# Normalising the second half of x during the projections, and spreading a stack's transfers over every second pair of maximum tiles

## The chip, the cores and the metric

The kernel runs on one core of a Trainium2 chip. A core has TensorE (PE, matmuls), VectorE (DVE), ScalarE (ACT), GpSimd (POOL) and SyncE (SP, which here only issues transfers), each with its own instruction stream that runs in order, an on-chip memory of 128 partitions, PSUM banks into which PE accumulates, and 16 DMA engines for transfers to and from DRAM. The metric is the device time of one execution in microseconds (us), less is better. Before the change it is 1792.7 us, the median of 3 runs (1792.57 to 1793.63).

## The reference

A block of multi-head attention and a token mixer, mixed by a gate. x is 2048 tokens by 640 channels, with 32 heads of 20 channels; the mixer's hidden width is 1728.

```python
def _A_ref(x, wqkv, wo):
    qkv = (x @ wqkv).reshape(B, S, 3, H, Dh).transpose(2, 0, 3, 1, 4)
    q, k, v = qkv[0], qkv[1], qkv[2]
    scores = jnp.einsum("bhqd,bhkd->bhqk", q, k) * (Dh ** -0.5)
    p = _softmax(scores, axis=-1)
    o = jnp.einsum("bhqk,bhkd->bhqd", p, v)
    return o.transpose(0, 2, 1, 3).reshape(B, S, D) @ wo

def _B_ref(x, w1, b1, w2, b2):
    h = _layernorm(x, axis=-1)
    u = _gelu(jnp.einsum("bsd,sf->bdf", h, w1) + b1)
    y = jnp.einsum("bdf,fs->bds", u, w2) + b2
    return y.transpose(0, 2, 1)

g = _sigmoid((x * gate_w).sum(-1, keepdims=True))
return g * _A_ref(...) + (1 - g) * _B_ref(...)
```

The change concerns h, the normalised x, in channels 320 to 639, and the order in which some operands are brought in.

## The kernel before

Every matmul that must be exact is done in three passes on a value split into a high and a low part (`hi_lo`: ACT rounds the high part, POOL or DVE subtracts for the low part). The program goes through four stages.

Projections (up to about 220 us of the profile): q, k and v from x. `qk_unit(m, q)` is one unit of 15 matmuls into one PSUM bank; four banks take turns, so a unit's bank is needed again four units later. ACT evicts the high part `evh`, DVE the low part `evl`, and SP stores both to DRAM. The last 24 units (n = 0 to 23) carry the preparation of the mixer's first half: for each tile t of 128 tokens, SP loads channels 0 to 319 of x (`h_load`, unit t + 1), POOL normalises them (`h_norm`, unit t + 2: add the negative mean, times the reciprocal deviation), ACT and POOL split them (`h_split`, unit t + 3) into `hh` and `hl`, which stay on the chip.

Mixer (about 220 to 740 us): twice, for d = 0 (channels 0 to 319) and d = 1 (320 to 639), 14 u tiles (hidden rows, one of them the 64-row tail of w1) and 16 y tiles (128 tokens each). The weights w1 and w2 come in pieces `wr` of 256 KB on SP's queue, about nine pieces ahead, and are split by ACT and POOL into `wh` and `wl` five pieces ahead. While the y tiles of d = 0 run, the second half of x is prepared: SP loads a tile (`h_load(1, t)`), DVE normalises it (`h_norm(1, t)`, 2500 ns of the planner's clock behind a y tile), ACT and POOL split it.

Into the mixer the program deals the first part of the next stage: maximum tiles. A softmax needs each query's maximum, so scores are computed once only for their maximum: PE makes a 128x512 score tile `s` (L208), ACT rectifies some of them (`s_over`, L223), and DVE takes the maxima (L214) or, in one operation, a sum and a maximum (L233). A head pair p has 128 such tiles. How many have been dealt by a step n of the mixer is set by `dve_room(n)`, a budget of DVE time that grows evenly over the mixer; during the y tiles of d = 0 it sets aside 600 ns a tile for the normalisation.

Each pair needs a stack: `load_stack` brings k and q, high and low parts, from DRAM into 120 rows, 21 transfers of 80 or 160 KB (`ks_False`, `qs_False`). In the mixer these transfers are not issued at once but put on the list `drip`, one of them taken with each pair of maximum tiles. At maximum tile 552 the stack of the attention loop's first pair (`ks_True`, `qs_True`) goes on the same list: 20 transfers, 8 of maxima from `m_d` and one of v (336 KB in runs of 168 bytes).

Attention loop (about 740 to 1745 us): scores, exponentials on ACT, probabilities times v on PE, with the remaining maximum tiles between. Then the last projection and the output.

Order: PE, ACT and DVE follow the order in which the program writes their instructions, POOL and SP too from the last 24 units on. An instruction that waits holds up all that stands behind it on its engine. A small planner (`act`, `later_on`, `settle`) orders ACT's and POOL's mixer work by due times on a clock of its own.

Of the kernel before, what the change touches and what calls it, by code (L numbers as in the profile page):

```python
# [7 lines left out]
F32 = mybir.dt.float32  # L8
F32R = mybir.dt.float32r
AF = mybir.ActivationFunctionType  # L10
OP = mybir.AluOpType
AX = mybir.AxisListType

P = 128
S, D, H, DH, F = 2048, 640, 32, 20, 1728
NP = H // 2
NT = S // P
NC = D // P
FF = 13
FT = 14  # L20
# [10 lines left out]
def gated_mix(ctx, tc, xT, x, wqk, wv0, wv1, wo, w1, w1t, b1, w2, b2, out):  # L31
# [31 lines left out]
    r_d = dram.tile([H, DH, S], F32, name="r_d")  # L63
    v_d = dram.tile([2, NT, P, 16 * VW], F32, name="v_d")
    y_d = dram.tile([S, D], F32, name="y_d")

    cp = ctx.enter_context(tc.tile_pool(name="cp", bufs=1))
    base = ctx.enter_context(tc.tile_pool(name="base", bufs=1))
# [45 lines left out]
    omg = cp.tile([P, NT], F32, name="omg")  # L114
    b2o = cp.tile([P, NT], F32, name="b2o")

    drip = []

    def load_stack(p, ks, qs, full, eng=nc.sync):
        put = eng.dma_start if eng else lambda *a: drip.append(lambda: nc.sync.dma_start(*a))  # L120
# [34 lines left out]

    s_src, st_src, v_tiles = {}, {}, {}

    def load_v(p):
        v_tiles[p] = base.tile([P, NT, NPAIR], F32, tag="v", bufs=2, name=f"v{p}")
        c0 = NPAIR * (p % 8)  # L160
        nc.sync.dma_start(v_tiles[p], v_d[p // 8, :, :, c0: c0 + NPAIR].rearrange("t p c -> p t c"))

    s_close = []

# [308 lines left out]

    def h_load(d, t):
        xm = hp.tile([P, HALF], F32, tag="xm", bufs=4, name=f"xm{d}_{t}")
        nc.sync.dma_start(xm, x[t * P:(t + 1) * P, d * HALF:(d + 1) * HALF])
        xms[d, t] = xm

    def h_norm(d, t):
        xm = xms[d, t]  # L480
        (nc.vector if d else nc.gpsimd).tensor_scalar(xm, xm, negm[:, t:t + 1], rstd[:, t:t + 1], op0=OP.add, op1=OP.mult)  # L481

    def h_split(d, t):
        xm = xms.pop((d, t))
# [60 lines left out]
    for n, (m, q) in enumerate(units):  # L545
        if n % 4 < 2 and n // 4 * 4 + 4 < len(units):
            m2 = units[n // 4 * 4 + 4][0]
            if n % 4 == 0:
                raws[m2] = w_dma(m2)
            else:  # L550
                w[m2] = load_w(m2, raws[m2])
        if n == 8:
            s_src[0] = base_stack(0, False, None)
        if 3 <= n < NT + 3:
            hs[n - 3] = h_split(0, n - 3)
        if 2 <= n < NT + 2:
            h_norm(0, n - 2)
        if 1 <= n < NT + 1:
            h_load(0, n - 1)
        if n == 17:  # L560
            w_raw(0)
            w_raw(1)
        last_stores = qk_unit(m, w[m], q)
        if n == 23:
            w_split(3)
        for _ in range(min(2, len(drip))):
            drip.pop(0)()
        if n in (18, 19):
            w_split(n - 18)
        if n in (20, 21):  # L570
            w_raw(n - 18)
        if n == 22:
            w_split(2)
            w_raw(4)
            w_raw(5)
# [17 lines left out]
    def later_on(delay, fn):  # L593
        events.append((clock[0] + delay, next(count), fn))
# [109 lines left out]
    def mlp(hs):  # L704
        k = 0
        for d in range(2):
            g, done = {}, set()
            for f in f_order:
                if d == 0 and f == f_order[-1]:
                    for i in range(3):  # L710
                        h_load(1, i)
                ps = mlp_tile(f"u{d}_{f}")
                for c in range(4):
                    wh, wl = w_need(k)
                    k += 1
                    for i in range(4):
                        force(lambda: hs.get(4 * c + i))
                        hh, hl = hs[4 * c + i]
                        ops = [(wh, hh), (wh, hl)] if f == FF else [(wh, hh), (wh, hl), (wl, hh)]
                        for n, (a, b) in enumerate(ops):  # L720
                            pair64(ps, a[:, i], b, c == i == n == 0, c == i == 3 and n == len(ops) - 1)
                            yield
                gh = gp.tile([P, HALF], F32R, tag=f"gh{f}", name=f"gh{d}_{f}")
                gl = None if f == FF else gp.tile([P, HALF], F32R, tag=f"gl{f}", name=f"gl{d}_{f}")
                u_evac(f, d, ps, gh, gl, done)
                g[f] = (gh, gl)
            for t in range(NT):
                ps = mlp_tile(f"y{d}_{t}")
                for c in range(4):
                    wh, wl = w_need(k)  # L730
                    k += 1
                    for i in range(4 if c < 3 else 2):
                        f = 4 * c + i
                        force(lambda: f in done)
                        gh, gl = g[f]
                        if f < FF:
                            for n, (a, b) in enumerate(((wh, gh), (wh, gl), (wl, gh))):
                                pair64(ps, a[:, i], b, f == n == 0, False)
                                yield
                        else:  # L740
                            nc.tensor.matmul(ps[0], wl[:TL, i], gh[:TL], start=False, stop=False)
                            pair64(ps, wh[:, i], gh, False, True)
                            yield
                y_evac(t, d, ps)
                if d and t == NT - 2:
                    act(lambda: nc.scalar.activation(eps_t, eps_t, AF.Exp), 1500, 1000, 8000)
                if d == 0:
                    if t == 0:
                        for i in range(NT):
                            hs[i] = None  # L750
                        h_norm(1, 0)
                    if t + 1 < NT:
                        later_on(2500, lambda t=t: h_norm(1, t + 1))

                    def split(t=t):
                        hs[t] = h_split(1, t)
                        if t + 3 < NT:
                            h_load(1, t + 3)

                    act(split, 370, 2000, 3000)  # L760
# [7 lines left out]

    hooks[0] = start_ahead
    FIRST = 14  # L770
    U_STEPS = (FT - 1) * 48 + 32
    DIFF, RAW, NORM = 435, 640, 600

    def dve_work(k):
        return DIFF * min(k, NDIFF * 128) + RAW * max(0, k - NDIFF * 128)

    def dve_room(n):
        norms = min(max((n - U_STEPS) / (NT * 40), 0), 1) * NT * NORM
        return (dve_work(S_AHEAD) + NT * NORM) * (n + 1 - FIRST) / (STEPS - 20 - FIRST) - norms

    first_p = {}

# [13 lines left out]
    for n, _ in enumerate(steps):  # L796
        if n == STEPS - 28:
            s_wide[0] = False
        if n in (STEPS - 22, STEPS - 16, STEPS - 10):
            first_scores((n + 22 - STEPS) // 6)  # L800
        settle(146)
        while done + 2 <= S_AHEAD and dve_work(done) < dve_room(n):
            if done == 48:
                s_src[1] = base_stack(1, False, None)
            if done == 4 * 128 + 40:
                st_src[0] = base_stack(0, True, None)
                for half in range(2):
                    load_m(0, st_src[0][1], half, lambda *a: drip.append(lambda: nc.sync.dma_start(*a)))
                drip.append(lambda: load_v(0))
            if drip:  # L810
                drip.pop(0)()
            for _ in range(2):
                s_next()
            done += 2
            settle(233)
# [345 lines left out]
```

## Time and profile before

| | |
|---|---|
| median of 3 runs | 1792.7 us |
| profiled execution: its time | 1796.82 us |
| profiled execution: its span | 1794.7 us |
| DVE normalisations (L481) in the mixer | 16, 14.1 us together |
| POOL normalisations (L481) in the projections | 16, 10.4 us together |
| DMA engines' mean busy share, 145 to 220 us | 0.85 |
| DMA engines' mean busy share, 580 to 590 us | 0.17 |

How to read the views shown below. A row of the groups gives line, engine, operation, what is written from what (buffer numbers left out), shapes and count, then busy time in us, mean ns of one, and the idle time just before with what ended it. A row of the stretches gives the bounds, the length, each engine's busy time with its instructions in brackets (PE, PE's weight loads PEld, DVE, ACT, POOL, as far as they occur), then PE's granted clock, the DMA engines' share and GB/s; cut down to one line of the program or one engine it shows fewer columns. A row of the timeline gives the start and the duration in us, and in square brackets how long the engine was idle before and what it waited for. A row of the transfers ends with the size in KB and the median us from issue to landing.

### The profile page before, as it was taken

The page shows a single profiled execution, that of the slowest core. Times are in us where ns is not written, and L with a number is a line of the kernel's source. Part 1 is how long each engine was busy: PE and PEld are TensorE (multiplying, and loading weights), DVE is VectorE, ACT ScalarE, POOL GpSimd, SP SyncE. Part 2 cuts the span into 40 slices and gives each one's busy share as a digit, 9 for nine tenths or more (in the row PEclk, how much of TensorE's full clock was granted, in tenths as well). Part 3 has the DMA queues.
Part 4 walks back from the last instruction along what each step waited for, and adds up shares of the span by engine and source line. Part 5 has one row for each costly group of instructions (what it writes and reads, how often), then busy time and mean ns, then how long its engine had stood idle before and what let it go on. Part 6 is the DMA issues. An engine that isn't in the chain of part 4 may idle for free.

```text
span 1794.7 us, 39876 instructions
## 1 busy us (share of the span) xinstructions
PE 1779.3 (99%) x14976; PEld 1113.8 (62%) x14976; DVE 1236.7 (69%) x2394; ACT 1481.1 (83%) x2534; POOL 640.7 (36%) x898
## 2 busy tenths in 40 slices
PE   9999999999999999999999999999999999999998
PEld 7998899999999999633333333333333333333388
DVE  5303289999889999777767677676777777767244
ACT  4244388887878886699999999999999999999930
POOL 1123377778877767211111111121332121212210
PEclk9999999999999999999999999999999999999999
DMA  8757876647675564325213223052363232301653
GB/s 292 241 173 245 258 188 170 161 152 193 175 180 161 144 183 142 90 57 131 59 30 82 61 68 83 18 105 70 46 138 69 52 86 59 73 13 25 216 154 125
DMA packets 157937, 222.95 MB, mean 124 GB/s; under 512 B 68590, under 2 KB 95614, under 8 KB 154318
## 3 DMA queue, kind: packets, MB, share of 16 engines
q1 hardware_dynamic: 139568, 190.74, 39.0%
q0 software_dynamic: 15440, 24.45, 5.8%
q10 hardware_dynamic: 2736, 5.21, 1.0%
q8 instruction: 118, 1.93, 0.5%
q14 instruction: 75, 0.61, 0.1%
HBM read 165.43 MB, written 54.54 MB: 123 GB/s over the span
## 4 chain that ended last, share of the span: by engine, by line
PE 93%; DVE 3%; DMA 3%; ACT 0%; issue 0%; SPq 0%; POOL 0%; ACTq 0%; DVEq 0%; POOLq 0%
PE pv L899 29%; PE st L986 20%; PE s L208 12%; PE u L48 10%; PE y L48 8%; PE qk L54 6%; PE v L54 4%; PE a L1066 3%; DVE mx L214 1%; DMA xr<-in_xT_dram 1%; DVE ov L233 1%; DVE oy L1072 1%; DVE xm L481 1%; DMA wr<-in_w_dram 0%; DMA rbl<-r_d 0%
## 5 line engine op out<-in xcount | busy, mean ns | idle before, releaser
L214 DVE TENSOR_REDUCE mx<-s 128x1 f32<-128x512 f32 x1280 | 834.4, 686 | 282.0 <-PE s L208 216.8
L1001 ACT ACTIVATE p<-st 128x512 f32<-128x512 f32 x1022 | 583.1, 657 | 1.1 <-PE st L986 1.1
L993 ACT ACTIVATE p<-st 128x1024 f32<-128x1024 f32 x511 | 552.4, 1081 | 2.8 <-PE st L986 2.2
L899 PE MATMUL pv<-p,v 128*32 128x512 f32 x4088 | 547.2, 605 | 0.0
L986 PEld LDWEIGHTS st<-qs_True,ks_True 62*128 62x128 f32 x2044 | 245.8, 184 | 432.1 <-ACT p L993 427.0
L986 PE MATMUL st<-qs_True,ks_True 62*128 62x512 f32 x2044 | 495.2, 446 | 0.0
L208 PE MATMUL s<-ks_False,qs_False 60*128 60x512 f32 x1152 | 340.1, 396 | 4.8 <-DVE mx L233 1.9
L43 POOL TENSOR_TENSOR wl<-wr,wh 128x512 fp32r<-128x512 f32 x228 | 275.5, 1219 | 80.3 <-ACT wh L40 64.8
L233 DVE CUSTOM_DVE_ANT_0 ov<-s,ov 128x512 f32<-128x512 f32 x384 | 263.6, 687 | 38.9 <-PE s L208 28.7
L223 ACT ACTIVATE ov<-s 128x512 f32<-128x512 f32 x384 | 226.4, 597 | 68.4 <-PE s L208 62.7
L208 PE MATMUL s<-sk,sq 60*128 60x512 f32 x896 | 279.7, 394 | 0.0
L879 POOL DMA_DIRECT2D l_d<-oev x128 | 62.7, 496 | 459.1 <-DVE oev L872 459.0
L48 PE MATMUL y<-gh,wh 64*128 64x320 f32 x896 | 223.1, 307 | 0.0
L48 PE MATMUL y<-gl,wh 64*128 64x320 f32 x832 | 214.7, 306 | 0.0
L48 PE MATMUL y<-gh,wl 64*128 64x320 f32 x832 | 214.1, 305 | 0.0
L208 PEld LDWEIGHTS s<-ks_False,qs_False 60*128 60x128 f32 x1152 | 190.0, 185 | 11.6 <-DVE mx L233 4.9
L899 PEld LDWEIGHTS pv<-p,v 128*32 128x32 f32 x4088 | 82.6, 108 | 174.9 <-issue 162.4
L40 ACT ACTIVATE wh<-wr 128x512 fp32r<-128x512 f32 (+3 forms) x247 | 147.0, 599 | 43.1 <-PE y L48 15.7
L48 PE MATMUL u<-hh,wh 64*128 64x320 f32 x864 | 178.7, 307 | 0.0
L48 PE MATMUL u<-hl,wh 64*128 64x320 f32 x864 | 178.6, 307 | 0.0
L208 PEld LDWEIGHTS s<-sk,sq 60*128 60x128 f32 x896 | 166.0, 185 | 18.1
L48 PE MATMUL u<-hh,wl 64*128 64x320 f32 x800 | 167.8, 307 | 0.0
(137 smaller groups left out, 2339.3 us busy)
## 6 DMA issues: line engine op xcount, KB each, us to landing
wr<-in_w_dram SPq DMA_DIRECT2D x192, 256.0 KB
ks_True<-k_d SPq DMA_DIRECT2D x96, 160.0 KB
qs_True<-q_d SPq DMA_DIRECT2D x192, 80.0 KB
qs_False<-q_d SPq DMA_DIRECT2D x108, 80.0 KB
sk<-k_d SPq DMA_DIRECT2D x42, 160.0 KB
sq<-q_d SPq DMA_DIRECT2D x84, 80.0 KB
v_d<-vt SPq DMA_DIRECT2D x32, 168.0 KB
v<-v_d SPq DMA_DIRECT2D x16, 336.0 KB
```

Source lines behind the costliest of these rows:

```text
L40: nc.scalar.activation(hi, src, AF.Copy)
L43: (lo_eng or nc.vector).tensor_sub(lo, src, hi.bitcast(F32))
L48: nc.tensor.matmul(ps[k], a[r], b[r], start=start, stop=stop)
L54: nc.tensor.matmul(ps, a, b, start=(i == 0 and k == 0), stop=(i == n - 1 and k == 2))
L208: nc.tensor.matmul(ps, qs[half][r, t * P:(t + 1) * P], ks[r, kc * 512:(kc + 1) * 512], start=True, stop=True)
L214: nc.vector.tensor_reduce(mx[:, slot, j, t: t + 1], ps, axis=AX.X, op=OP.max)
L223: nc.scalar.activation(over[j, kc], ps, AF.Relu)
L233: nc.vector.tensor_tensor_reduce(ov, ps, ov, 1.0, -3.0e38, OP.add, OP.max, mx[:, slot, j, t: t + 1])
L899: nc.tensor.matmul(pv[r: r + 32, :], v_tiles[p][:, kt, 10 * j: 10 * j + 32], pt[j, c], start=(kt == 0), stop=(kt == NT - 1))
L986: nc.tensor.matmul(ps, ks[r, kt * P:(kt + 1) * P], qs[qh][r, c * 512:(c + 1) * 512], start=True, stop=True)
L993: nc.scalar.activation(pt, ps, AF.Exp, scale=SCALE)
L1001: nc.scalar.activation(pt, ps, AF.Exp, scale=SCALE)
```

## The change

Three things are altered.

The second half of x is normalised during the last 24 projection units and kept in DRAM, in the new array `xn_d`. For tile t, POOL issues a load of x's channels 320 to 639 into one of three buffers (`n_load`, unit t + 2), DVE normalises in place (`n_store`, unit t + 4), and POOL issues the store to `xn_d`. In the mixer `h_load(1, t)` reads `xn_d` in place of x, and the 16 DVE normalisations there are gone.

The budget for maximum tiles no longer sets time aside for them, so that it grows evenly over the whole mixer.

A stack's transfers are taken from `drip` with every second pair of maximum tiles (after the first 128 tiles). Those for the attention loop's first pair go on a second list, `slow`, taken with the pairs between, and the first v comes in 8 transfers of 42 KB.

```diff
+    xn_d = dram.tile([S, HALF], F32, name="xn_d")
...
-    drip = []
+    drip, slow = [], []
...
-    def load_v(p):
+    def load_v(p, pieces=1, put=nc.sync.dma_start):
         v_tiles[p] = base.tile([P, NT, NPAIR], F32, tag="v", bufs=2, name=f"v{p}")
         c0 = NPAIR * (p % 8)
-        nc.sync.dma_start(v_tiles[p], v_d[p // 8, :, :, c0: c0 + NPAIR].rearrange("t p c -> p t c"))
+        for i in range(pieces):
+            kt = slice(i * NT // pieces, (i + 1) * NT // pieces)
+            put(v_tiles[p][:, kt], v_d[p // 8, kt, :, c0: c0 + NPAIR].rearrange("t p c -> p t c"))
...
-        nc.sync.dma_start(xm, x[t * P:(t + 1) * P, d * HALF:(d + 1) * HALF])
+        rows = slice(t * P, (t + 1) * P)
+        nc.sync.dma_start(xm, xn_d[rows] if d else x[rows, :HALF])
...
-    def h_norm(d, t):
-        xm = xms[d, t]
-        (nc.vector if d else nc.gpsimd).tensor_scalar(xm, xm, negm[:, t:t + 1], rstd[:, t:t + 1], op0=OP.add, op1=OP.mult)
+    def h_norm(t):
+        xm = xms[0, t]
+        nc.gpsimd.tensor_scalar(xm, xm, negm[:, t:t + 1], rstd[:, t:t + 1], op0=OP.add, op1=OP.mult)
+
+    xns = {}
+
+    def n_load(t):
+        xns[t] = hp.tile([P, HALF], F32, tag="ty", bufs=3, name=f"xn1_{t}")
+        nc.gpsimd.dma_start(xns[t], x[t * P:(t + 1) * P, HALF:])
+
+    def n_store(t):
+        xn = xns.pop(t)
+        nc.vector.tensor_scalar(xn, xn, negm[:, t:t + 1], rstd[:, t:t + 1], op0=OP.add, op1=OP.mult)
+        nc.gpsimd.dma_start(xn_d[t * P:(t + 1) * P], xn)
...
         if 2 <= n < NT + 2:
-            h_norm(0, n - 2)
+            h_norm(n - 2)
+        if 4 <= n < NT + 4:
+            n_store(n - 4)
+        if 2 <= n < NT + 2:
+            n_load(n - 2)
...
-                        h_norm(1, 0)
-                    if t + 1 < NT:
-                        later_on(2500, lambda t=t: h_norm(1, t + 1))
...
-    U_STEPS = (FT - 1) * 48 + 32
-    DIFF, RAW, NORM = 435, 640, 600
+    DIFF, RAW = 435, 640
...
     def dve_room(n):
-        norms = min(max((n - U_STEPS) / (NT * 40), 0), 1) * NT * NORM
-        return (dve_work(S_AHEAD) + NT * NORM) * (n + 1 - FIRST) / (STEPS - 20 - FIRST) - norms
+        return dve_work(S_AHEAD) * (n + 1 - FIRST) / (STEPS - 20 - FIRST)
...
             if done == 4 * 128 + 40:
+                held, drip[:] = list(drip), []
                 st_src[0] = base_stack(0, True, None)
+                put = lambda *a: drip.append(lambda: nc.sync.dma_start(*a))
                 for half in range(2):
-                    load_m(0, st_src[0][1], half, lambda *a: drip.append(lambda: nc.sync.dma_start(*a)))
-                drip.append(lambda: load_v(0))
-            if drip:
+                    load_m(0, st_src[0][1], half, put)
+                load_v(0, 8, put)
+                slow[:], drip[:] = drip, held
+            if drip and (done % 4 == 0 or done < 128):
                 drip.pop(0)()
+            elif slow and done % 4 == 2:
+                slow.pop(0)()
```

How the change moves instructions, at three places. The first is POOL in the last projection units, tiles 1 to 3 of x (`xm` is the first half's tile, `xn` the second half's, `hl` the low part). Before:

```order
L481 TENSOR_SCALAR xm_1_1499<-xm_1_1499,negm,rstd 128x320
L43 TENSOR_TENSOR hl_1_1555<-xm_1_1499,hh_1_1554 128x320
L481 TENSOR_SCALAR xm_2_1528<-xm_2_1528,negm,rstd 128x320
L43 TENSOR_TENSOR hl_2_1590<-xm_2_1528,hh_2_1589 128x320
L481 TENSOR_SCALAR xm_3_1559<-xm_3_1559,negm,rstd 128x320
L43 TENSOR_TENSOR hl_3_1627<-xm_3_1559,hh_3_1626 128x320
```

With the change:

```order
L485 TENSOR_SCALAR xm_1_1502<-xm_1_1502,negm,rstd 128x320
L491 DMA xn_1_1531<-in_x_dram 128x320
L43 TENSOR_TENSOR hl_1_1560<-xm_1_1502,hh_1_1559 128x320
L485 TENSOR_SCALAR xm_2_1533<-xm_2_1533,negm,rstd 128x320
L496 DMA xn_d<-xn_0_1500 128x320
L491 DMA xn_2_1566<-in_x_dram 128x320
L43 TENSOR_TENSOR hl_2_1599<-xm_2_1533,hh_2_1598 128x320
L485 TENSOR_SCALAR xm_3_1568<-xm_3_1568,negm,rstd 128x320
L496 DMA xn_d<-xn_1_1531 128x320
L491 DMA xn_3_1605<-in_x_dram 128x320
L43 TENSOR_TENSOR hl_3_1640<-xm_3_1568,hh_3_1639 128x320
```

Between a normalisation and the subtraction now stand a store, which waits for DVE, and a load, which from tile 3 on waits until the store of three tiles before has landed.

The second is DVE at the same units (`evl` is the low part of q or k, `wl` that of a weight, `kf` a copy or difference of keys). Before:

```order
L43 TENSOR_TENSOR evl_3_1547<-qk_3_1530,evh_3_1546 128x512
L43 TENSOR_TENSOR evl_0_1578<-qk_0_1561,evh_0_1577 128x512
L330 COPY kf_0_1583<-qk_0_1561 128x512
L43 TENSOR_TENSOR wl_1586<-wr_1552,wh_1585 128x640
L43 TENSOR_TENSOR evl_1_1613<-qk_1_1596,evh_1_1612 128x512
```

With the change:

```order
L43 TENSOR_TENSOR evl_3_1552<-qk_3_1535,evh_3_1551 128x512
L495 TENSOR_SCALAR xn_0_1500<-xn_0_1500,negm,rstd 128x320
L43 TENSOR_TENSOR evl_0_1587<-qk_0_1570,evh_0_1586 128x512
L333 COPY kf_0_1592<-qk_0_1570 128x512
L43 TENSOR_TENSOR wl_1595<-wr_1557,wh_1594 128x640
L495 TENSOR_SCALAR xn_1_1531<-xn_1_1531,negm,rstd 128x320
L43 TENSOR_TENSOR evl_1_1626<-qk_1_1609,evh_1_1625 128x512
```

Ahead of each unit's eviction now stands a normalisation, which waits for the load on POOL's queue.

The third is SP in the mixer, second half, where the maxima of the first attention stack come in (`wr` is a weight piece). Before:

```order
L512 DMA wr_8465<-in_w_dram 128x512
L120 DMA qs_True_8057<-q_d 20x1024 x2
L808 DMA qs_True_8056<-m_d 1x32x32
L512 DMA wr_8521<-in_w_dram 128x512
L808 DMA qs_True_8056<-m_d 1x32x32 x3
L512 DMA wr_8576<-in_w_dram 128x512
```

With the change:

```order
L527 DMA wr_8850<-in_w_dram 128x512
L691 DMA sw_8877<-xg_13_8792 64x320
L692 DMA sw_8877<-xg_13_8792 64x320
L822 DMA qs_True_8022<-m_d 1x32x32
L527 DMA wr_8898<-in_w_dram 128x512
L822 DMA qs_True_8022<-m_d 1x32x32
L527 DMA wr_8953<-in_w_dram 128x512
L822 DMA qs_True_8022<-m_d 1x32x32
L121 DMA ks_False<-kd_d 20x1024
L822 DMA qs_True_8022<-m_d 1x32x32
L527 DMA wr_9018<-in_w_dram 128x512
```

Two weight pieces had up to three of the stack's transfers between them; now mostly one, and for the time in which the next score stack overlaps, two or three again.

## The prediction

> **What bounds the kernel now.** I read the page's busy shares first, then its chain of waits.
>
> ```profile
> PE 1779.3 (99%) x14976; PEld 1113.8 (62%) x14976; DVE 1236.7 (69%) x2394; ACT 1481.1 (83%) x2534; POOL 640.7 (36%) x898
> PE 93%; DVE 3%; DMA 3%; ACT 0%; issue 0%; SPq 0%; POOL 0%; ACTq 0%; DVEq 0%; POOLq 0%
> ```
>
> TensorE (PE) is hardly ever idle, so the question is where its matmuls come more slowly than they could. The next view cuts the mixer (220 to 740 us) into stretches of 10 us; in each row the numbers after "PE busy" are its microseconds and, in brackets, its matmuls.
>
> ```profile
> 380.00:390.00 10.00, 10.00 (x126) 9.85 (x124) 8.96 (x23) 7.66 (x16) 8.55 (x9) 1.00 0.51 156
> 410.00:420.00 10.00, 9.55 (x116) 9.00 (x112) 9.15 (x22) 8.24 (x17) 8.56 (x9) 1.00 0.84 196
> 440.00:450.00 10.00, 9.81 (x122) 9.51 (x122) 8.96 (x21) 8.05 (x17) 8.37 (x9) 1.00 0.56 165
> 500.00:510.00 10.00, 10.00 (x121) 9.63 (x119) 8.72 (x25) 7.05 (x17) 5.97 (x11) 1.00 0.77 155
> 510.00:520.00 10.00, 8.67 (x103) 8.03 (x101) 7.24 (x18) 7.69 (x17) 6.41 (x6) 1.00 0.64 171
> 520.00:530.00 10.00, 9.93 (x117) 9.20 (x115) 8.31 (x21) 7.36 (x15) 6.41 (x6) 1.00 0.87 239
> 530.00:540.00 10.00, 10.00 (x125) 10.00 (x123) 9.22 (x26) 8.49 (x19) 9.55 (x13) 1.00 0.73 187
> ```
>
> Undisturbed, PE does 125 or 126 matmuls in 10 us. There are two dips: a shallow one from 390 to 470, a deep one from 500 to 530. The attention loop behind the mixer, which makes up the rest of the span, can begin only when it ends, so a microsecond won there is won at the end.
>
> **The shallow dip is the normalisation on VectorE (DVE).** The rows below are the first evacuation of five y tiles (ScalarE, L701), then the neighbourhood of one normalisation.
>
> ```profile
> 375.42 0.61 ACT L701 ACTIVATE ty<-y,b2o,omg 128x320 f32<-128x320 f32 x1
> 383.24 0.61 ACT L701 ACTIVATE ty<-y,b2o,omg 128x320 f32<-128x320 f32 x1
> 390.79 0.61 ACT L701 ACTIVATE ty<-y,b2o,omg 128x320 f32<-128x320 f32 x1
> 473.02 0.62 ACT L701 ACTIVATE ty<-y,b2o,omg 128x320 f32<-128x320 f32 x1
> 480.84 0.62 ACT L701 ACTIVATE ty<-y,b2o,omg 128x320 f32<-128x320 f32 x1
> ...
> 393.06 1.30 POOL L43 TENSOR_TENSOR wl<-wr,wh 128x512 fp32r<-128x512 f32 x1 [2.15 <-ACT wh L40]
> 393.43 1.10 DVE L481 TENSOR_SCALAR xm<-xm,negm,rstd 128x320 f32<-128x320 f32 x1
> 395.20 0.49 PE L208 MATMUL s<-ks_False,qs_False 60*128 60x512 f32 x1 [0.18 <-DVE mx L233]
> ```
>
> A y tile takes 7.82 us (375.42 to 383.24, 473.02 to 480.84), but the ten tiles from 390.79 to 473.02 take 82.23 us, 4.0 more than ten times 7.82. In them the normalisation begins while GpSimd (POOL) subtracts (393.06 plus 1.30 is 394.36) and ends 0.17 us behind it; DVE is late by as much, and PE waits for a score's buffer at 395.20. The Trainium skill ("SBUF — State Buffer", section "SBUF: two separate sides") says that such a DVE instruction and a GpSimd one hold a port pair exclusively, each for its whole length; these two rows agree.
>
> **Term 1: the 16 normalisations leave the mixer.** The 4.0 us go, since nothing takes their place: the planner now deals 17.2 maximum tiles to a y tile of the first half, where 16.2 stand now (157 in 80 us, below, times 8.28 us for a tile), and as many fewer elsewhere, so PE's matmuls are the same in sum. That so many maxima by themselves do not stall PE is shown by the second half's y tiles, which have 17.6 (67 in 30 us) and run at 7.91 us (79.07 us for ten).
>
> ```profile
> 390.00:470.00 80.00, 53.69 (x157) 28.64 (x156) 1.00 0.64 180
> 640.00:670.00 30.00, 21.76 (x67) 12.11 (x66) 1.00 0.66 184
> ...
> 623.81 0.61 ACT L701 ACTIVATE ty<-y,b2o,omg 128x320 f32<-128x320 f32 x1
> 702.88 0.62 ACT L701 ACTIVATE ty<-y,b2o,omg 128x320 f32<-128x320 f32 x1
> ```
>
> I take -4.0; between 0 (if the denser maxima stall as the norms did) and -4.0.
>
> **Term 2: the stacks' transfers are thinned out.** The rows show how the deep dip begins.
>
> ```profile
> 514.13 0.63 ACT L40 ACTIVATE wh<-wr 128x512 fp32r<-128x512 f32 x1 [0.86 <-DMA wr<-in_w_dram]
> 514.67 0.58 ACT L223 ACTIVATE ov<-s 128x512 f32<-128x512 f32 x1
> 515.30 0.50 PE L208 MATMUL s<-ks_False,qs_False 60*128 60x512 f32 x2 [1.02 <-ACT ov L223]
> ```
>
> A weight piece lands late, ScalarE waits for it, the rectified score (L223) behind it is late, and PE waits for that score's buffer. From 500 to 530 the three rows have 4, 22 and 8 matmuls fewer than 125, 34 times 80 ns (10 us by 125), 2.7 us. The late piece stood on SyncE (SP) among two or three of a stack's transfers to a piece; at this tile it is now mostly one, and the large load of v comes later and in eighths. I take -2.2, not all, since the tile of w1's tail that uses up its weights faster stays there; between 0 and -2.7.
>
> **Term 3: what the projections take on.** Into 145 to 220 us come 16 loads and 16 stores of 160 KB on POOL's queue and 16 normalisations on DVE.
>
> ```profile
> 145.00:220.00 75.00, 75.00 (x324) 60.50 (x322) 21.61 (x30) 24.06 (x46) 28.84 (x35) 1.00 0.85 264
> L481 DVE TENSOR_SCALAR xm<-xm,negm,rstd 128x320 f32<-128x320 f32 x16 | 14.1, 882 | 0.0
> 62.80 0.55 POOL L334 DMA_DIRECT2D kd_d<-evl  x1 [2.22 <-DVE evl L43]
> L43 POOL TENSOR_TENSOR hl<-xm,hh 128x320 fp32r<-128x320 f32 x16 | 14.6, 914 | 16.3 <-ACT hh L40 16.3
> L481 POOL TENSOR_SCALAR xm<-xm,negm,rstd 128x320 f32<-128x320 f32 x16 | 10.4, 648 | 36.2 <-DMA xm<-in_x_dram 36.2
> ```
>
> DVE goes from 21.6 to 35.7 of 75 us busy, POOL from 28.8 to 46.4 (32 issues of 0.55): by work alone hidden under PE's 75. Two things are not.
>
> The transfers: 264 GB/s at a share of 0.85 is 311 GB/s at full share. 75 us of 264 GB/s are 19.8 MB; 5.2 MB more make 25.0 MB, which take 80 us, 5 more than there are. The Trainium skill ("DMA: Bandwidth & Descriptors", section "Specifications") gives some 358 GB/s from memory to a core; by that estimate the 25.0 MB take 70 us, nothing is short, and the sum below would lose its term 3. The 311 is from this stage's own mixture, so I use it.
>
> The order on POOL: a load waits until the store of three tiles before has landed, and that store stood one tile earlier in POOL's order.
>
> ```profile
> kd_d<-evl POOLq DMA_DIRECT2D x4, 256.0 KB, 5.8
> xn<-in_x_dram POOLq DMA_DIRECT2D x16, 320.0 KB, 4.1
> wor<-in_wo_dram POOLq DMA_DIRECT2D x5, 320.0 KB, 7.7
> ```
>
> A loop over two tiles is thus one landing L, a load's issue 0.55, the subtraction 0.91 and the other half's normalisation 0.65. With L at 5.6, a little below the 256 KB store's 5.8, that is 7.7 us for two tiles, 3.85 for one; PE has a unit in 3.49 (216.53 to 220.02, below). What is queued behind a waiting load is POOL's subtraction and the next normalisation of the first half; ScalarE's high part waits for that one, an eviction stands behind it in ScalarE's order, and PE needs the evicted bank four units later.
>
> ```profile
> 156.06 1.18 POOL L481 TENSOR_SCALAR xm<-xm,negm,rstd 128x320 f32<-128x320 f32 x1
> 208.18 0.61 POOL L481 TENSOR_SCALAR xm<-xm,negm,rstd 128x320 f32<-128x320 f32 x1 [5.52 <-DMA xm<-in_x_dram]
> 208.83 0.47 ACT L40 ACTIVATE hh<-xm 128x320 fp32r<-128x320 f32 x1 [5.95 <-POOL xm L481]
> 209.82 0.69 DVE L43 TENSOR_TENSOR evl<-qk,evh 128x512 fp32r<-128x512 f32 x1 [4.79 <-ACT evh L40]
> 216.53 0.60 ACT L40 ACTIVATE evh<-qk 128x512 fp32r<-128x512 f32 x1 [2.90 <-PE qk L54]
> 220.02 0.60 ACT L40 ACTIVATE evh<-qk 128x512 fp32r<-128x512 f32 x1 [2.37 <-PE qk L54]
> ```
>
> The tightest place is the last tile: its normalisation starts at 208.18, unit 18's bank is free at 210.51, and unit 22, which needs it, starts at 216.53 less 3.49, 213.04. So 2.5 us are left. With 3.85 a tile, POOL by itself would be at that instruction 159 plus 11 times 3.85, 201 (the fourth tile's normalisation, 156.06, has behind it the first load that waits; 1.18, 0.55 and 0.91 later, at about 159, comes the fifth's, and the last is 11 tiles on). That is earlier than the landing that it waits for anyway. What remains is the 5 us of missing transfer time. If they fell on the last tile whole, PE would stall 5 less 2.5, 2.5 us; if earlier gaps take them, not at all. I take +1.5; between 0 and +8 (the long landings below).
>
> **Sum.** -4.0 - 2.2 + 1.5 = -4.7 us. The profiled execution's span of 1794.7 becomes 1790.0 and its own time of 1796.8 becomes 1792.1. That execution stands 4.1 above the median of the runs, 1792.7, so I forecast **1788.0 us**. 0.2% (3.6 us) is about what a measurement can tell from no change: below 1789.1 is faster, above 1796.3 slower.
>
> **Rivals.**
>
> A, slower: landings on POOL's queue become the projections' pace. For: 26% more bytes (5.2 on 19.8 MB) in an already full stage, and 7.7 us for wo's load on that queue. Against: 4.1 and 5.8 for its others. The loop's share per tile is half of L plus 2.1; 159 plus 11 times that reaches 210.7 (208.18 plus 2.5) at L = 7.3. From there each microsecond of L costs 5.5 us, the 6.2 won are gone at 8.4, and 9.2 gives 10.5 of stall: 1797.0. The page on SBUF named above adds that a DMA's descriptors on POOL's queue cannot be written while a normalisation holds the ports. By that rule, at 0.6 us a tile, PE would stall from L = 6.1 and the gain be gone at 7.2; no row of before has such a pair.
>
> B, weights late all the same: at 500 to 530 it is the w1 tail's pace, not the stack. For: the dip lies at that tile. Against: the first half has the tile too, without a dip. -4.0 + 1.5: 1790.2, which a measurement hardly tells.
>
> C, the gain of term 1 is eaten: the denser maxima, on a DVE that is 90% busy, delay PE's buffers as the norms did. Against: the second half's y tiles. -2.2 + 1.5: 1792.0.
>
> D, nothing at all is lost in the projections and the deep dip goes whole: -6.7, 1786.0.
>
> **Chances.** Forecast 0.48 (0.43 of it beyond 0.2%), A 0.20 (0.16 slower, 0.04 within), B 0.20, C 0.07, D 0.05. So faster 0.48, same 0.36, slower 0.16. The forecast's own range is 1785.5 to 1790.5. The whole range goes from 1784.5, below D, to 1797.0, A's price; it leaves out A's worse half.
>
> **What would show it.** Term 1: y tiles of the first half all at 7.8 to 8.0 us, 125 or 126 matmuls in each 10 us from 390 to 470. Term 2: no wait of PE for L223 behind a late weight, 120 or more matmuls from 510 to 530. Term 3: the first mixer matmul, now at 220, no later than 223, POOL's new stores landing in 7 us or less, and DVE not waiting long for the new load. Idle PE between 150 and 222, or a mixer that starts at 228, would prove A; a new dip at 390 to 470 without norms would prove C. I am wrong in kind if the mixer ends no earlier relative to its start.

## The result, and the profile after

| | before | after |
|---|---|---|
| median of 20 runs each | 1794.76 us | 1798.85 us |
| lowest and highest | 1792.57, 1798.14 | 1792.46, 1803.48 |
| ratio of the runs, 95% interval | | 1.0021 [1.0014, 1.0027] |
| profiled execution: span, mean granted clock | 1794.7 us, 0.999 | 1790.6 us, 1.000 |

The change makes the kernel slower by 0.21%, some 4 us. The profiled execution of after is the fastest of its 20 runs, and the only one at a clock of 1.000; the other 19 have 0.996 to 0.999 (all 20 together 0.9974 on average). So the profile alone would mislead here: its span is 4.1 us shorter than before's.

The mixer is what the prediction hoped for. The stretches of after (PE busy, PE's weight loads, DVE, ACT, POOL, then clock, DMA share, GB/s):

```profile
145.00:220.00 75.00, 72.00 (x306) 56.67 (x305) 30.60 (x44) 22.83 (x44) 44.96 (x66) 1.00 0.94 304
220.00:230.00 10.00, 7.38 (x69) 6.34 (x69) 3.83 (x6) 3.61 (x8) 2.58 (x2) 1.00 0.97 336
...
410.00:420.00 10.00, 10.00 (x127) 9.91 (x126) 8.75 (x24) 8.54 (x18) 9.60 (x13) 1.00 0.73 217
440.00:450.00 10.00, 10.00 (x128) 10.00 (x126) 8.94 (x23) 8.22 (x16) 8.55 (x10) 1.00 0.67 207
510.00:520.00 10.00, 10.00 (x124) 10.00 (x123) 8.86 (x22) 9.09 (x19) 7.31 (x8) 1.00 0.94 228
520.00:530.00 10.00, 10.00 (x126) 10.00 (x124) 9.08 (x24) 8.11 (x17) 8.40 (x10) 1.00 0.69 188
```

Where before had 116, 122, 103 and 117 matmuls (410, 440, 510 and 520) there are 127, 128, 124 and 126: both dips are gone. The price stands in the first two rows. From 145 to 220 PE does 306 matmuls where it did 324; at 75 us by 324, 0.23 us each, that is 4.2 us. The DMA share there rose from 0.85 to 0.94. PE's waits from 130 to 245 us (total, times, longest; before has none there):

```profile
PE qk L54 <- DVE evl L43: 3.0, 4, 1.7
PE s L211 <- ACT ov L226: 2.6, 1, 2.6
```

The 3.0 us come through DVE's order. Each of the four evictions `evl` that PE waits for stands right behind a normalisation that has waited for its own load on POOL's queue, and that load is what ended the wait. The longest of the four, and then all that DVE waits for these loads from 130 to 235 us:

```profile
206.22 0.45 DVE L495 TENSOR_SCALAR xn<-xn,negm,rstd 128x320 f32<-128x320 f32 x1 [4.28 <-DMA xn<-in_x_dram]
206.58 0.68 DVE L43 TENSOR_TENSOR evl<-qk,evh 128x512 fp32r<-128x512 f32 x1
207.41 0.47 PE L54 MATMUL qk<-xh,wh 128*128 128x512 f32 x1 [1.69 <-DVE evl L43]
```

```profile
DVE xn L495 <- DMA xn<-in_x_dram: 24.6, 10, 4.3
```

For the evictions' own stores DVE waits only 4.2 us there, where it waited 20.6 before. What made the 2.6 us is seen on ScalarE, and the last row is PE's:

```profile
219.60 0.60 ACT L40 ACTIVATE evh<-qk 128x512 fp32r<-128x512 f32 x1 [3.29 <-DMA q_d<-evh]
222.65 0.60 ACT L40 ACTIVATE evh<-qk 128x512 fp32r<-128x512 f32 x1 [2.46 <-DMA q_d<-evh]
226.32 0.60 ACT L40 ACTIVATE evh<-qk 128x512 fp32r<-128x512 f32 x1 [2.56 <-DMA k_d<-evh]
228.82 1.09 ACT L226 ACTIVATE ov<-s 128x512 f32<-128x512 f32 x2 [1.38 <-DMA k_d<-evh]
...
229.47 0.50 PE L211 MATMUL s<-ks_False,qs_False 60*128 60x512 f32 x1 [2.62 <-ACT ov L226]
```

The last evictions of the projections wait for q's and k's own stores to land and give back a buffer. The last one of them ran at 220.80 in the profile of the thinned transfers alone (thin, below), 1.0 us behind its matmuls; here it comes at 226.32, 4.0 behind (PE's first mixer matmul is at 219.8 there, at 222.4 here). The rectified scores stand behind it in ScalarE's order, and PE waits for their bank. So some of the stage's old stores were needed before they had landed. The profile gives no time from issue to landing for them (they are on SP's queue), so it doesn't tell whether they were issued later or took longer.

**The sum of this pair of profiles.** The mixer, from its first matmul to the first score of the attention loop, took 515.9 us (219.9 to 735.8) and takes 511.7 (222.4 to 734.1), 2.6 of them that wait: 6.8 won. The projections and the wait cost 4.2 plus 2.6, 6.8 too. Of the other 4 us of the spans, 3.6 stand at places that the change doesn't alter:

```profile
0.00:40.00 40.00, 36.63 (x140) 28.21 (x141) 23.54 (x38) 19.48 (x34) 7.20 (x16) 0.96 0.84 285
```

```profile
PE a L1066 <- DVE oy L1072: 3.5, 8, 1.7
```

```profile
0.00:40.00 40.00, 37.31 (x147) 28.43 (x148) 24.53 (x39) 21.26 (x37) 8.05 (x17) 1.00 0.86 300
```

```profile
PE a L1085 <- DVE oy L1091: 1.7, 7, 0.3
```

The first two rows (a stretch, and one of PE's waits over the span) are before's, the other two after's. Before's execution had a clock of 0.96 in its first 40 us and did 7 matmuls fewer (at 0.26 us, 1.8 us), and waited 1.8 us longer at its very end. On these terms the two profiles show next to no difference. But the profile of after is its fastest run, 6.4 us below its median, and the slower runs have a lower clock. What that clock has to do with the change is what the experiments had to find besides the cause of the late landings.

### The profile page after: what moved, and what is told of

Same layout as the page of the kernel before. It is cut to its first block, busy times and chain, and to the rows that moved or that the text cites. A ratio compares the mean times of both kernels' runs of the same rounds, so it can differ in the third digit from the quotient of the medians.

```text
span 1790.6 us, 39960 instructions
## 1 busy us (share of the span) xinstructions
PE 1775.7 (99%) x14976; PEld 1111.3 (62%) x14976; DVE 1236.9 (69%) x2394; ACT 1482.0 (83%) x2534; POOL 656.7 (37%) x930
## 3 DMA queue, kind: packets, MB, share of 16 engines
HBM read 168.05 MB, written 57.16 MB: 126 GB/s over the span
## 4 chain that ended last, share of the span: by engine, by line
PE 93%; DMA 5%; DVE 1%; issue 0%; POOL 0%; SPq 0%; ACT 0%; ACTq 0%; DVEq 0%; POOLq 0%
PE pv L918 29%; PE st L1005 21%; PE s L211 12%; PE u L48 11%; PE y L48 10%; PE v L54 4%; PE a L1085 4%; PE qk L54 3%; DMA wr<-in_wqk_dram 1%; DMA xm<-in_x_dram 1%; DMA xr<-in_xT_dram 1%; DMA wr<-in_w_dram 1%; DVE oy L1091 0%; DMA kd_d<-kf 0%; DMA xn_d<-xn 0%
```

## The experiments

Two theories for the loss in the projections: the **bytes** (5.2 MB more in a stage whose DMA engines are almost full make its transfers land late), or the **order** (loads, stores and normalisations that wait in POOL's and DVE's order, which is rival A's loop). Ratios are to the kernel before, run beside them; its medians were 1796.15, 1793.86 and 1794.97 us in the three groups.

### The two parts apart

**thin**: before, with only the stacks' transfers and v as in the change.

```diff
-            if drip:
+            if drip and (done % 4 == 0 or done < 128):
                 drip.pop(0)()
+            elif slow and done % 4 == 2:
+                slow.pop(0)()
```

> The kernel before, with the thinned stack transfers and the v in eighths alone (no xn_d; DVE normalises in the mixer as before). Theory P (the mixer's two dips were cured, worth 6.7 us, and the projections gave back more): only the dip of 500 to 530 goes, the ten y tiles of 8.28 us stay; about 2.7 us less than the kernel before, ratio 0.9985 (0.998 to 0.9995). Rival Z (the thinned transfers themselves cost time, at the end of the mixer or in the attention loop): slower than before, ratio 1.001 or more.

Measured: 1792.1 us, ratio 0.9986 [0.9977, 0.9995], as expected. **norm**: the change with these lines, `load_v` and its call as before.

> The change without its transfers' part (a stack's transfers with every pair, v in one piece). Theory P: the y tiles run at 7.9 us, the dip of 500 to 530 is there as before, PE idles and starts the mixer late at 200 to 232; ratio to before 1.003 to 1.0045 (4.0 won, about 10.8 lost). Rival Z: no slower than before, ratio 0.998 to 1.000.

Measured: 1805.09 us, ratio 1.0056 [1.0042, 1.0071], more than the expected 1.003 to 1.0045. Stretches of thin:

```profile
410.00:420.00 10.00, 9.60 (x116) 9.05 (x112) 9.16 (x22) 8.22 (x17) 8.55 (x9) 1.00 0.57 172
510.00:520.00 10.00, 10.00 (x126) 9.97 (x124) 8.90 (x23) 9.49 (x21) 8.75 (x8) 1.00 0.86 219
```

And of norm:

```profile
410.00:420.00 10.00, 10.00 (x127) 9.96 (x125) 9.05 (x27) 8.94 (x19) 8.53 (x11) 1.00 0.69 185
510.00:520.00 10.00, 9.30 (x111) 8.65 (x109) 7.95 (x21) 7.13 (x16) 4.92 (x6) 1.00 0.63 156
```

Each part cures its own dip and leaves the other. The loss belongs to the normalisation's part alone, which by itself is 9 us slower than before by the medians.

### Bytes or order

**bytes**: no load, no wait, and the second half of x is left unnormalised; a copy within DRAM on POOL's queue takes the place of load and store. It reads and writes as many bytes of DRAM (168.05 and 57.16 MB in the profiles of both kernels), but they pass the DMA engines once and not twice: 2.6 MB in place of 5.2.

```diff
     def n_load(t):
-        xns[t] = hp.tile([P, HALF], F32, tag="ty", bufs=3, name=f"xn1_{t}")
-        nc.gpsimd.dma_start(xns[t], x[t * P:(t + 1) * P, HALF:])
+        pass
 
     def n_store(t):
-        xn = xns.pop(t)
-        nc.vector.tensor_scalar(xn, xn, negm[:, t:t + 1], rstd[:, t:t + 1], op0=OP.add, op1=OP.mult)
-        nc.gpsimd.dma_start(xn_d[t * P:(t + 1) * P], xn)
+        nc.gpsimd.dma_start(xn_d[t * P:(t + 1) * P], x[t * P:(t + 1) * P, HALF:])
```

> The change, but the second half of x goes from DRAM to DRAM unnormalised, one 160 KB copy a tile on POOL's queue: the same bytes, no waits of POOL and none of DVE (the normalisation of the second half is left out). Theory P-bytes (the full DMA engines slow the projections): mixer starts at 224 to 232 us as in the changed kernel, ratio to before 1.001 to 1.003. Theory P-order (the waits in POOL's and DVE's order slow them): projections as before, mixer starts at 220 to 222, ratio 0.996 to 0.997.

**order4**: all instructions and waits of the change, on 4 of the 320 columns; the mixer loads x itself (a line not shown), so that its second half is left unnormalised.

```diff
-        xns[t] = hp.tile([P, HALF], F32, tag="ty", bufs=3, name=f"xn1_{t}")
-        nc.gpsimd.dma_start(xns[t], x[t * P:(t + 1) * P, HALF:])
+        xns[t] = hp.tile([P, 4], F32, tag="tz", bufs=3, name=f"xn1_{t}")
+        nc.gpsimd.dma_start(xns[t], x[t * P:(t + 1) * P, HALF:HALF + 4])
...
-        nc.gpsimd.dma_start(xn_d[t * P:(t + 1) * P], xn)
+        nc.gpsimd.dma_start(xn_d[t * P:(t + 1) * P, :4], xn)
```

> The change, but the load, the normalisation and the store of the second half take 4 of the 320 columns, and the mixer loads x itself (its second half stays unnormalised): the same instructions and waits, hardly any bytes. Theory P-order: mixer starts at 224 to 232 us, ratio to before 1.001 to 1.003. Theory P-bytes: mixer starts at 220 to 222, ratio 0.996 to 0.997.

**bufs6**: the change with six buffers for the tile instead of three.

```diff
-        xns[t] = hp.tile([P, HALF], F32, tag="ty", bufs=3, name=f"xn1_{t}")
+        xns[t] = hp.tile([P, 512], F32, tag="over", bufs=3, name=f"xn1_{t}")[:, :HALF] if t % 2 else hp.tile([P, HALF], F32, tag="ty", bufs=3, name=f"xn1_{t}")
```

> The change with six buffers for the second half's tile where it has three, so that a load no longer waits for the store of three tiles before to land. Theory B (the bytes; the transfers are as many): nothing is won, ratio 1.000 to 1.004, the mixer starts at 222 or later. Theory O (rival A as the prediction had it, the loop over landing, load and subtraction): the stalls go, the mixer starts at 220 to 221, ratio 0.996.

| | us | ratio | PE's waits, 130 to 245 us | mean clock of the runs |
|---|---|---|---|---|
| bytes | 1797.38 | 1.0012 [0.9999, 1.0024] | gaps of 2.2 and 2.2 | 0.9976 |
| order4 | 1787.91 | 0.9964 [0.9951, 0.9977] | none | 0.9983 |
| bufs6 | 1800.5 | 1.0032 [1.0021, 1.0044] | gaps of 3.1 and 2.6 | 0.9963 |

The order alone costs nothing: order4 has every issue and every wait (DVE waits 19.7 us for the small loads, POOL 7.0 us for the small stores), and its time is the lowest of the study. The copies alone bring back most of the loss. Looser waits do not help: in bufs6 POOL no longer waits for a store to land (in after it does, 7 times, 10.9 us in all), and it is as slow as the change beside it (again, below, 1.0037). So the cause is what the new transfers move and not the order in which they are issued; by which wait it reaches PE differs, through DVE's normalisations in the change and in bufs6, through the evictions' own stores in bytes. That the order adds to the bytes isn't excluded (bytes 1.0012, the change 1.0021 and 1.0037), nor that the second pass through the DMA engines does.

### How many bytes, and where

**half**: every second tile of bytes only, and the mixer's loads to match (that line is not shown).

```diff
     def n_store(t):
+        if t % 2:
+            return
         nc.gpsimd.dma_start(xn_d[t * P:(t + 1) * P], x[t * P:(t + 1) * P, HALF:])
```

> The bytes alone, halved: only every second tile of x's second half is copied within DRAM on POOL's queue during the projections (8 copies of 160 KB), the mixer loads the other tiles from x; the second half is not normalised at all. By the prediction's own sum of bytes (19.8 MB plus 2.6 are 22.4 MB, 72 us at 311 GB/s, of 75) nothing is short: the mixer starts at 220 to 221, no idle gap of PE over 1 us, clock 1.00 from 200 to 250, ratio 0.996 to 0.997. If the loss goes with the bytes one by one, half of the gap between the order alone and the bytes: ratio 0.9988.

**late**: all copies, with the mixer's weight pieces instead of the projections' units.

```diff
     def w_need(k):
+        if 10 <= k < 10 + 3 * NT and k % 3 == 1:
+            n_store((k - 10) // 3)
...
-        if 4 <= n < NT + 4:
-            n_store(n - 4)
```

> All 16 copies of the second half of x within DRAM, but issued in the mixer's first 130 us, one with every third weight piece, where the DMA engines are busy 0.5 to 0.7 of the time; the second half is not normalised. If it is the fullness of the projections and not the bytes as such: no stall of PE in 200 to 250, ratio 0.996 to 0.997. If the bytes hurt anywhere (weights late behind them): matmuls below 120 in some 10-us rows of 245 to 340, ratio 0.998 to 1.001.

Measured: half 1795.11 us, ratio 0.9998 [0.9987, 1.0009]; late 1790.2 us, 0.9976 [0.9965, 0.9988], with 125 to 127 matmuls in every 10 us from 230 to 330 and the copies in place. The same copies are nearly free where the mean DMA share is 0.63 without them (before, 230 to 360 us) and 0.67 with them. But half of them, beside it, already cost 4.9 us of the median against late; the first expectation for half (nothing is lost) missed, and the second, 0.9988, lies at the edge of the interval. So the loss may grow faster than the bytes at first, or in step with them; these runs don't decide it.

In half's profile nothing is lost until the mixer starts (326 matmuls from 145 to 220, before 324). Then PE waits 2.8 us for a rectified score, as in the change, because ScalarE waits for stores of the evictions. DVE's and ScalarE's waits for these stores from 130 to 235 us, before:

```profile
DVE evl L43 <- DMA q_d<-evl: 11.9, 6, 2.9
DVE evl L43 <- DMA k_d<-evl: 8.7, 3, 3.1
```

half:

```profile
DVE evl L43 <- DMA k_d<-evl: 13.1, 4, 4.1
DVE evl L43 <- DMA q_d<-evl: 12.6, 5, 3.7
ACT evh L40 <- DMA q_d<-evh: 4.5, 2, 2.7
```

bytes:

```profile
DVE evl L43 <- DMA q_d<-evl: 17.0, 6, 5.3
DVE evl L43 <- DMA k_d<-evl: 14.6, 4, 5.1
ACT evh L40 <- DMA q_d<-evh: 6.4, 3, 2.6
```

and late, which has no copy in that stage:

```profile
DVE evl L43 <- DMA k_d<-evl: 14.4, 5, 4.0
DVE evl L43 <- DMA q_d<-evl: 14.1, 6, 4.2
```

DVE's sums are 20.6, 25.7, 31.6 and 28.5 us. They do not tell the kernels apart: late's is larger than half's, and PE waits for nothing in it. Nor does the mean DMA share from 145 to 220, 0.86 in half, which loses time, and 0.87 in order4 and late, which do not. What tells them apart is whether a wait is long enough, and late enough in the stage, to reach PE. So that the copies cost time in this stage is shown; how they delay the other transfers is not.

### The clock behind a gap

**again** is the changed kernel once more.

> The changed kernel itself once more. Theory B (the projections lack transfer time, PE stands idle for two to three us between 200 and 230, and after such a gap the granted clock falls to about 0.5 for some 4 us): ratio to before 1.001 to 1.003 again; if its profile has an idle gap of 2.2 us or more, the 2-us windows behind it show a clock of 0.5 to 0.8, and the mean clocks of its runs lie below those of before. Theory O (it is the order on POOL and DVE alone, and the clock has nothing to do with it): the same ratio, but the clock behind the gaps is 1.00 and the mean clocks are those of before.

Measured: 1801.26 us, ratio 1.0037 [1.0024, 1.005], mean clock 0.9968. Its profile, in stretches of 2 us:

```profile
206.00:208.00 2.00, 0.27 (x1) 0.30 (x2) 1.47 (x3) 0.52 (x2) 1.13 (x2) 1.00 1.03 350
208.00:210.00 2.00, 2.00 (x6) 1.34 (x5) 1.98 (x3) 0.60 (x1) 1.42 (x3) 0.54 0.88 151
210.00:212.00 2.00, 2.00 (x7) 1.54 (x6) 0.35 (x1) 0.00 (x0) 0.00 (x0) 0.61 0.97 214
212.00:214.00 2.00, 2.00 (x10) 1.64 (x9) 0.00 (x0) 1.01 (x3) 1.14 (x2) 1.00 1.02 387
...
230.00:232.00 2.00, 0.17 (x2) 0.17 (x4) 1.85 (x4) 0.82 (x2) 0.00 (x0) 1.00 0.95 361
232.00:234.00 2.00, 2.00 (x15) 2.00 (x17) 1.04 (x4) 1.79 (x4) 1.14 (x1) 0.51 0.57 161
234.00:236.00 2.00, 2.00 (x21) 2.00 (x19) 1.21 (x4) 0.60 (x1) 1.39 (x2) 0.63 0.90 265
```

PE stands idle for 2.1 us, and then works for 4 us at 0.54 and 0.61 of its clock; again for 3.3 us, and 0.51 and 0.63 follow. Each such fall costs 2 us times the missing 0.46 and 0.39, 1.7 us, on top of the gap. The two falls make 3.4 us, about the 3.6 by which this span is longer than after's, in which PE waits as long (5.6 us from 130 to 245, here 5.7) and the clock doesn't fall; but the two executions differ elsewhere as well (141 and 147 matmuls in the first 40 us). (In bufs6 the falls were longer, 0.50 in three stretches of 2 us running.) To see whether the gap alone does it, a copy of the mixer's first weight piece onto itself holds PE up, with no byte more: once behind the last eviction (**gap2**), or six times before it (**gap1**).

```diff
         if n == 23:
             w_split(3)
+            wh0 = w_got[0][0]
+            nc.scalar.activation(wh0, wh0.bitcast(F32), AF.Copy)
```

> The thinned transfers alone, and one more activation on ScalarE that copies the first weight piece of the mixer onto itself, placed so that PE's first mixer matmul comes some 2.6 us late; no byte more is moved. Theory G (an idle gap of more than about 2 us by itself lets the granted clock fall to about 0.5 for some 4 us): the 2-us windows behind the gap show a clock of 0.5 to 0.8 in at least some of the profiles, PE loses 2.6 plus about 2 us, ratio 1.001 (0.9986 of the thinned transfers alone plus 0.0025), and the mean clocks of the runs are 0.996 to 0.999. Theory H (the fall belongs to the full DMA engines, not to the gap): clock 1.00 behind the gap, a loss of 2.6 us, ratio 1.000.

> The same with six copies placed earlier on ScalarE, so that PE's first mixer matmul comes only some 1.3 us late. Theory G: a gap this short leaves the clock at 1.00, the loss is the gap alone, ratio 0.9993, mean clocks 0.999 as with the thinned transfers alone. If also short gaps cost clock: windows of 0.5 to 0.8 behind it, ratio 1.000 or more.

Measured: gap2 1795.33 us, ratio 1.0001 [0.9991, 1.0011]; gap1 1795.04 us, 0.9995 [0.9984, 1.0006]. The profile of gap2, and PE's wait in it:

```profile
220.00:222.00 2.00, 0.44 (x5) 0.47 (x7) 1.22 (x2) 1.46 (x3) 0.98 (x1) 0.97 1.01 347
222.00:224.00 2.00, 2.00 (x18) 2.00 (x18) 0.00 (x0) 0.00 (x0) 0.31 (x1) 0.50 1.08 336
224.00:226.00 2.00, 2.00 (x23) 2.00 (x21) 0.00 (x0) 0.17 (x1) 0.00 (x0) 0.68 1.02 285
```

```profile
PE u L48 <- issue: 1.8, 1, 1.8
```

and of gap1:

```profile
222.00:224.00 2.00, 0.83 (x4) 0.35 (x2) 0.69 (x1) 1.91 (x4) 0.00 (x0) 1.00 0.94 265
224.00:226.00 2.00, 1.58 (x22) 1.61 (x23) 0.69 (x1) 1.33 (x3) 0.59 (x1) 1.00 1.09 324
```

```profile
PE u L48 <- issue: 1.6, 1, 1.6
```

The gaps came out at 1.8 and 1.6 us, nearer to each other than meant, so the two times say little: gap2's is what was expected without a fall, 1.000, though its profile has one. The rows say more: the clock falls to 0.50 behind an ordinary gap of 1.8 us, without the new bytes. The DMA engines are full at that place in all kernels, so this pair does not rule them out, though thin, which has shares of 1.03 and 0.99 from 220 to 224 and no gap, keeps a clock of 1.00. That full engines are not needed is seen at another place, the end of the mixer, where PE waits once for a maximum while the DMA engines hardly work. In order4:

```profile
732.00:734.00 2.00, 0.71 (x6) 0.23 (x2) 1.77 (x4) 1.42 (x2) 0.00 (x0) 1.00 0.00 0
734.00:736.00 2.00, 1.85 (x11) 0.53 (x11) 1.86 (x3) 0.69 (x2) 0.00 (x0) 0.83 0.49 172
736.00:738.00 2.00, 2.00 (x10) 0.83 (x6) 0.00 (x0) 0.42 (x1) 0.00 (x0) 0.50 0.67 160
```

```profile
PE s L211 <- DVE mx L217: 1.3, 1, 1.3
```

Here the share is 0.00 during a gap of 1.3 us, and the clock falls to 0.50 all the same. All 14 profiles have this gap, of 1.3 or 1.7 us, the kernel before too; behind 8 of them the clock fell, and not in before, after, again, thin, norm and bytes. Over all profiles PE had 13 more gaps of 1.6 us or more between 195 and 236 us; behind 9 of them it fell, and it did not behind those of 1.6 (gap1), 1.7 and 2.6 (after) and one of 2.1 (norm). A gap makes the fall possible, not certain, and between 1.3 and 2.6 us its length does not decide it. The Trainium skill ("TensorE: Matmul & The Clock Gate", section on the clock gate in Part 1) says that the clock is halved after at least one idle window of some 3.4 us, and that the window runs freely; the half agrees with these rows and the chance in it may be that window's, the length does not agree: 1.3 us were enough.

### Two kernels without the bytes

Both keep the thinned transfers and the even budget, and normalise the second half in the mixer again, on another engine than DVE. **poolnorm** uses POOL:

```diff
-        (nc.vector if d else nc.gpsimd).tensor_scalar(xm, xm, negm[:, t:t + 1], rstd[:, t:t + 1], op0=OP.add, op1=OP.mult)
+        nc.gpsimd.tensor_scalar(xm, xm, negm[:, t:t + 1], rstd[:, t:t + 1], op0=OP.add, op1=OP.mult)
```

> The thinned transfers, and the second half of x loaded and normalised in the mixer as before, but on POOL instead of DVE; nothing is kept in DRAM. If the shallow dip came only from DVE being held up by POOL's subtraction: the dip goes without the price in the projections, ratio 0.996 to 0.997 (1789 against 1796), 125 or 126 matmuls per 10 us from 390 to 470, mixer start at 220. If the dip comes from a normalisation and maxima side by side on the shared ports, wherever the normalisation runs: 116 to 124 matmuls remain in several of these rows, ratio 0.998 to 0.999, like the thinned transfers alone.

**actnorm** uses ScalarE, where the high part is made; `nmr` is negm times rstd (lines of the planner that go with it are not shown):

```diff
+            nc.scalar.activation(xm, xm, AF.Identity, bias=nmr[:, t:t + 1], scale=rstd[:, t:t + 1])
```

> The thinned transfers, and the second half of x loaded and normalised in the mixer on ScalarE (bias and scale of one activation), in one piece with its high part. ScalarE is 83% busy over the span, and 16 times about 0.47 us more is 7.5 us of 230: if there is room, ratio 0.996 to 0.997 with 125 or 126 matmuls per 10 us from 390 to 470; if ScalarE's evictions of the scores (L223) or of y come late for it, 116 to 123 matmuls in some of these rows and a ratio of 0.998 to 1.001.

Measured: poolnorm 1788.5 us against 1793.86, ratio 0.9972 [0.9961, 0.9984]; actnorm 1792.1 us, 0.9988 [0.9977, 0.9998]. poolnorm beats both kernels. Its row of the shallow dip, and its normalisations from 380 to 480 us:

```profile
410.00:420.00 10.00, 10.00 (x128) 9.96 (x127) 8.83 (x24) 8.26 (x17) 9.68 (x11) 1.00 0.62 189
```

```profile
L483 POOL TENSOR_SCALAR xm<-xm,negm,rstd 128x320 f32<-128x320 f32 x12 | 7.4, 615 | 0.0
```

Before, the same stretch had them on DVE:

```profile
L481 DVE TENSOR_SCALAR xm<-xm,negm,rstd 128x320 f32<-128x320 f32 x12 | 11.6, 964 | 0.0
```

On POOL they stand in one line with its subtractions and take 0.62 us instead of 0.96; on DVE they ran beside them and were held up. actnorm has 123 and 120 matmuls in its rows at 410 and 430, in the range that was expected if ScalarE becomes late; its profile shows no wait of PE there, so the reason is not shown. poolnorm and actnorm hold the thinned transfers too, which alone gave 0.9986.

## Why the prediction was wrong

I forecast 1788.0 us, 0.26% faster than the median shown; the kernel is 0.21% slower. Of the 10.9 us between 1788.0 and 1798.85, 2.1 are the kernel before itself, whose median was 1792.7 in 3 runs and 1794.76 in 20.

- **The two dips and what makes them: right.** Each went with the part of the change that term 1 and term 2 put it down to (thin, norm).
- **Terms 1 and 2, -4.0 and -2.2: right in place, a little small.** Together 6.8 us are won in the mixer, against 6.2. B (weights late all the same) falls with 124 matmuls at 510, C (denser maxima) with 127 and 128 at 410 and 440.
- **Term 3, +1.5: this step failed.** It measured 4.2 us in the projections and 2.6 behind them, 6.8 in the one profile at full clock, and more in the other runs. Two things in its working were wrong. The sum of the bytes (25.0 MB at 311 GB/s, 5 us short, 2.5 of them taken by slack) treats the stage as one pipe that is either short or not; half loses time where that sum has 7 us to spare (19.8 plus 1.3 MB through the DMA engines, 68 us at 311 GB/s; its expectation counted the copies twice). The page of the Trainium skill that I weighed against it there ("DMA: Bandwidth & Descriptors", 358 GB/s, nothing short) would have been further off. And only POOL's order was followed for slack. DVE was counted by its work alone, though a normalisation that waits for its load now stands ahead of each eviction: that wait is 24.6 us, and through it came the 3.0 us that PE waits in the projections. That DVE would not wait long for the new load was named as a sign and did not hold, while the two beside it did (the mixer starts at 222.4, POOL's stores land in 5.1 us). The other path left out is ScalarE's: its evictions wait for their own stores, three buffers deep, and from there came the 2.6 us behind the projections.
- **Rival A: right in the sign, half right in the mechanism.** Its loop on POOL needs landings of 7.3 us. They took 5.1 in the median and 6.8 at most:

```profile
xn<-in_x_dram POOLq DMA_DIRECT2D x16, 160.0 KB, 5.1
xn_d<-xn POOLq DMA_DIRECT2D x16, 160.0 KB, 5.1
```

  POOL did wait for its stores (10.9 us), but that loop is not what costs: without these waits bufs6 is as slow, and with them order4 loses nothing. The same goes for a longer loop that the prediction left out, from a load over its normalisation, its store and the next load into the same buffer: two landings of 5.1, 0.94 on DVE and two issues of 0.54 and 0.58 make 4.1 us for one of its three tiles, an estimate, where PE has a unit in 3.49; six buffers halve it and win nothing. What held of it is its first reason, 26% more bytes in a stage that is already full, and that landings on POOL's queue reach PE, by DVE's order. Its proof as I had put it, idle PE between 150 and 222, did come, but it shows that the projections are late, not why.
- **What no step had: the price of a gap in clock.** I counted idle time at its own length. A gap can cost 1.7 us more. The mean clock of after's 20 runs is 0.9974 where before's was 0.9990 (26 runs beside bytes and order4): 0.0016 of 1795 us are 2.9 us. With the sum of 0 on equal terms that makes 2.9, against 4.1 measured in the medians (interval 2.5 to 4.8). This is an estimate from runs of different groups, and not all of the clock belongs to the two new gaps: order4, which has neither, has 0.9983, and in its profile the clock falls at the mixer's end. Behind which gaps the clock fell in the runs without a profile isn't known.

Left open: how the copies delay the stage's other transfers; how much of the 4.1 us the falls of the clock make; and which of the late stores a further eviction buffer would cover, and whether the change could be kept with one, was not tried.

## What to carry to other kernels

Before moving work into a stage, look at its DMA share and not only at its engines: at 0.85 here it had no room for more, and what pays is whatever waits for a landing ahead of other work on an engine that runs in order, new loads and old stores alike. An instruction that another engine's work holds up may be better put behind that work on the same engine (poolnorm) than carried through memory. And compare the mean clocks of all runs before believing one profile: a short gap in TensorE's work may cost as much again.

## What the runs showed that I had not expected

- TensorE's granted clock can fall to about half for some 4 us behind idle gaps as short as 1.3 us, with the DMA engines idle too: it did behind 17 of the 27 gaps above. A fall costs 1.7 us or more.
- Sixteen copies of 160 KB cost 9.5 us of the median in a stage at a share of 0.85 (bytes against order4, 1797.38 and 1787.91), and in a stage at 0.63 little or nothing (late, 0.9976, against 0.9964, within their intervals).
- Eight of them in the first stage, 1.3 MB through the DMA engines, already cost 4.9 us (half against late, 1795.11 and 1790.2), and the mean share there is no higher (0.86 and 0.87).
